# Three-operation weight decoding: a separate tile for signs and low bits, GpSimd as first reader, earlier release of raw tiles, and weights stored tile by tile

## The chip, the cores and the metric

The kernel runs on one core of one Trainium2 chip. The metric is the device time in microseconds (us) of one execution. TensorE (PE) does the matmuls, VectorE (DVE), ScalarE (ACT) and GpSimd (POOL) the elementwise work, and SyncE (SP) issues the DMA transfers.

## What is computed

Attention with a memory term, then two feed-forward blocks, on 2304 tokens of width 512:

```python
scores = softmax(causal(q @ k.T / 8))          # 4 batches, 8 heads, 576 tokens, 64 wide
attn = g * (phi(q) @ M_prev) / (phi(q) @ z_prev) + (1 - g) * (scores @ v)
x = attn.transpose(0, 2, 1, 3).reshape(2304, 512)
x = (((x @ w1) * (x @ w2)) @ w3) @ w_out       # d_ff = 1024
h = x @ w_in                                   # d_ff = 2048
out = (h - np.tanh(h)) @ wo2
```

All inputs but the weights are float32; the weights come as float64 (the scale factors promote them), as 64-bit words in memory. The kernel therefore decodes each float64 into float32 on the chip, and splits that into a rounded high part and a low rest, so that a product costs three fast matmuls (high by high, high by low, low by high).

## The kernel before

**Stages.** In the first some 260 us the attention runs: 80 units (16 head pairs by 5 query blocks), each scores on PE, row maximum on DVE, exponential on ACT, scaling on POOL (line 369), transposes and products on PE. Beside it, as background work, w3 and w_out are folded into one matrix (`fold_work`), which takes 24 decoded weight tiles. Then come six groups of 384 tokens (`for g in range(6)`): for each of eight column blocks f, PE forms `x @ w1` and `x @ w2` (tile ab), ACT copies (line 652), DVE multiplies (653), ACT rounds (656), DVE takes the rest (657), and PE multiplies by the folded matrix two blocks later (`x2_pe`, tile x). The memory term of the next group (`mem_group`, tile mw) runs beside them on all engines. From about 620 us the last block runs: 96 steps of `h2_pe` and `out_pe`.

**Decoding.** 72 tiles of 128 by 512 weights are decoded by `dec_ops`, a generator whose `yield`s cut it into steps. A raw tile holds the 64-bit words; `hw` is the upper half of each word, `lw` the lower, so both are read with 8 bytes from one element to the next. Before the change a tile takes: ACT scales `hw` into tile T (line 77) and writes rounded low bits, 16 bits each, into the raw tile (78); POOL clamps T (80) and writes the sign, again 16 bits each, into the raw tile (81); DVE shifts T by three and ORs it with the raw word (85). For a "whole" item this ends in the destination. For the others, POOL rounds to the high part (97) and DVE or POOL subtracts (100).

**Decoders.** A `Decoder` holds a list of items, steps up to `width` of them in turn, and calls `load` (SP issues the transfer, line 68) while items loaded and active are fewer than `ahead`. There are four: that of the fold (width 1, ahead 3), `wd` for w1 and w2 (16 items; width 2, ahead 3; the first four early, the rest in the first token group, where PE's block f asks for items 2f and 2f+1), `pre` for 24 whole items of the last block (width 2, ahead 2; 14 of them in the first two groups, ten later), and `fd` for its last eight (width 2, ahead 2, after 570 us). Raw tiles have three buffers, T two.

**Order.** The instructions are laid out by a list scheduler at build time, which takes the program's order as priority and gives tiles their buffers; on the chip each engine then works through its own fixed list in order, and SP's list of transfers is fixed too.

Of the kernel before, what the change touches and what calls it, by code (L numbers as in the profile page):

```python
# [11 lines left out]
F32 = mybir.dt.float32  # L12
F32R = mybir.dt.float32r
BF16 = mybir.dt.bfloat16
U32 = mybir.dt.uint32
U16 = mybir.dt.uint16
F16 = mybir.dt.float16
I64 = mybir.dt.int64
AF = mybir.ActivationFunctionType
ALU = mybir.AluOpType  # L20
# [1 line left out]
PSUM = bass.MemoryType.PSUM  # L22

REBIAS = 2.0 ** -112
TOP = float(np.uint32((255 << 20) - 1).view(np.float32))
LOW_SCALE, LOW_BIAS = 0.89 * 2.0 ** -29, 0.375


# [6 lines left out]
def block_kernel(ctx, tc, qk, qt, vt, mp, zp_d, beta, w1, w2, w3t, wo, wi, wo2, ident_d, mask_d, out):  # L35
    nc = tc.nc
    PE, DV, AC, PO, SP = nc.tensor, nc.vector, nc.scalar, nc.gpsimd, nc.sync
# [6 lines left out]
    zp = ctx.enter_context(tc.tile_pool(name="zp", bufs=1, side="right"))  # L44
    stg = {"raw": ctx.enter_context(tc.tile_pool(name="draw", bufs=3, side="right")),
           "T": ctx.enter_context(tc.tile_pool(name="dT", bufs=2, side="right"))}


    ident = cp.tile([128, 128], F32, name="ident")
    identb = cp.tile([128, 128], BF16, name="identb")  # L50
    maskb = cp.tile([128, 192], BF16, name="maskb")
    gates = cp.tile([128, 8], F32, name="gates")
    omg = cp.tile([128, 8], F32, name="omg")
    omgt = cp.tile([128, 4], F32, name="omgt")
# [7 lines left out]

    def dec_load(src):
        raw = stg["raw"].tile([128, 512], I64, tag="raw", name="raw")
        dst = raw[:]
        if len(src.shape) == 3:
            dst = dst.rearrange("p (k n) -> p k n", k=src.shape[1])
        SP.dma_start(out=dst, in_=src)
        return raw

    def dec_ops(raw, dst, lo_on, whole, hip):
        r16 = raw[:].bitcast(U16).rearrange("p (n t) -> p n t", t=4)
        rb = raw[:].bitcast(U32).rearrange("p (n t) -> p n t", t=2)
        lw, hw = rb[:, :, 0], rb[:, :, 1]
        t = stg["T"].tile([128, 512], U32, tag="T", name="T")
        tf = t[:].bitcast(F32)
        AC.activation(out=tf, in_=hw.bitcast(F32), func=AF.Copy, scale=REBIAS)  # L77
        AC.activation(out=r16[:, :, 0], in_=lw, func=AF.Copy, scale=LOW_SCALE, bias=LOW_BIAS)  # L78
        yield
        PO.tensor_scalar(out=tf, in0=tf, scalar1=TOP, scalar2=-TOP, op0=ALU.min, op1=ALU.max)  # L80
        PO.tensor_scalar(out=r16[:, :, 1].bitcast(F16), in0=hw.bitcast(F32), scalar1=2.0 ** -100, scalar2=2.0 ** -53,  # L81
                         op0=ALU.mult, op1=ALU.mult)
        yield
        o = dst() if whole else t[:]
        DV.scalar_tensor_tensor(out=o, in0=t, scalar=3, in1=lw,
                                op0=ALU.logical_shift_left, op1=ALU.bitwise_or)
        if whole:
            return
        yield
        hi, lo = dst()  # L90
        nhi[0] += 1
        if hip == 3:
            hip = nhi[0] % 2
        if hip == 2:
            DV.tensor_copy(out=hi, in_=tf)
        elif hip:
            PO.tensor_scalar(out=hi, in0=tf, scalar1=1.0, scalar2=1.0, op0=ALU.mult, op1=ALU.mult)
        else:
            AC.activation(out=hi, in_=tf, func=AF.Copy)
        lo_on.tensor_tensor(out=lo, in0=tf, in1=hi.bitcast(F32), op=ALU.subtract)  # L100

    class Decoder:


        def __init__(self, items, width, ahead, lo_on=DV, whole=False, hip=None):
            self.todo, self.loaded, self.active = deque(items), deque(), deque()
            self.width, self.ahead, self.done, self.total, self.lo_on = width, ahead, 0, len(self.todo), lo_on
            self.whole, self.hip = whole, HIP if hip is None else hip
            self.load()

        def load(self):
            while self.todo and len(self.loaded) + len(self.active) < self.ahead:
                src, dst = self.todo.popleft()
                self.loaded.append((dec_load(src), dst))

        def step(self):
            while self.loaded and len(self.active) < self.width:
                raw, dst = self.loaded.popleft()
                self.active.append(dec_ops(raw, dst, self.lo_on, self.whole, self.hip))
            if not self.active:  # L120
                return False
            gen = self.active.popleft()
            if next(gen, 1) is None:
                self.active.append(gen)
            else:
                self.done += 1
                self.load()
            return True

        def pump(self, n):  # L130
# [44 lines left out]
    for x in PA:  # L175
        apl[x] = att.enter_context(tc.tile_pool(name="ap" + x, bufs={"1": 1, "2": 2, "r": RB,
                                                                     "3": 1 if PU else PB, "4": 6}[x]))
    ap1, ap2, apr, ap3, ap4 = [apl[x] for x in "12r34"]
    V = [ap1.tile([128, 5, 2, 64], F32, name=f"v{i}") for i in range(2)]

    qk_t = {}
# [28 lines left out]
    def fold_o_item(j):  # L210
        def dst():
            FO[j] = slot(otags[j])
            return FO[j][:, 0], FO[j][:, 1]

        return wo[j * 128:j * 128 + 128], dst

    def fold_item(f, half):
        def dst():
            t = wslot(ap1, "zs")
            fv[f, half] = t  # L220
            return t[:, 0], t[:, 1]

        r = slice(512 * half, 512 * half + 512)
        return w3t[r, f * 128:f * 128 + 128].rearrange("(k p) c -> p k c", p=128), dst

    def fold_work(psum):
        seq = [("o", j) for j in range(4)]
# [39 lines left out]
    if True:  # L267
# [176 lines left out]
        def w_item(w, W, x, f):  # L444
            def dst():
                W[f] = slot(f"{x}{f}")
                return W[f][:, 0], W[f][:, 1]

            return w[:, f * 128:f * 128 + 128].rearrange("(k p) f -> p k f", p=128), dst

        wdec = [None]
        w_items = [w_item(w, W, x, f) for f in range(8) for w, W, x in ((w1, W1, "wa"), (w2, W2, "wb"))]
# [234 lines left out]
        pre_t = {}  # L687

        def fin_src(j):
            f = j // 2  # L690
            return (wo2[f * 128:f * 128 + 128] if j % 2
                    else wi[:, f * 128:f * 128 + 128].rearrange("(k p) f -> p k f", p=128))

        def fin_item(j):
            def dst():
                t = fslot(free.popleft())
                fin_tiles[j] = t[:, 0], t[:, 1]
                return fin_tiles[j]

            return fin_src(j), dst  # L700
# [50 lines left out]
        for g in range(6):  # L751
            for f in range(8):
                wd.until(2 * f + 2)
                o = ab_pe(xl, f)
                ab_chain(g, f, o)
                for y in [(g - 1, 7)] if f == 0 and g else [(g, 5), (g, 6)] if f == 7 else [(g, f - 2)] if f >= 2 else []:
                    x2_pe(*y)
                if f >= 1:
                    if g == 5:
                        if f == 1:  # L760
                            pre.until(2 * NF)
                            fd = Decoder([fin_item(j) for j in range(2 * NF, 32)], 2, 2, PO, False, HF)
                        left += [f"wa{f - 1}", f"wb{f - 1}"] + [f"wf{f - 3}"] * (f >= 3)
                        while plan and len(left) >= (2 if plan[0] == "P" else 1):
                            if plan.pop(0) == "P":
                                place(placed, [left.pop(0), left.pop(0)])
                                placed += 1
                            else:
                                give([left.pop(0)])
                    if g == 0:  # L770
                        wd.until(2 * f + 4)
                for _ in range(MS):
                    mem_step()
                if wd.done == 16:
                    if pre is None:
                        order = [*range(NZ), *range(NF, NF + NZ), *range(NZ, NF), *range(NF + NZ, 2 * NF)]
                        pre = Decoder([pre_item(j) for j in order], 2, 2, DV, True)
                    for _ in range(FS if g < 5 else FS5):
                        if pre.done < allowed:
                            pre.step()  # L780
                        elif fd and fd.done < given:
                            fd.step()
            if g + 1 < 6:
                mem_until(g + 1)
            xl = stage((g + 1) % 6)
        x2_pe(5, 7)
        pB.close()


        c2 = ctx.enter_context(tc.tile_pool(name="c2", bufs=2))  # L790
# [141 lines left out]

def layout(q, k, v, M_prev, z_prev, beta, moe_w1, moe_w2, moe_w3, moe_w_out, moe2_w_in, moe2_w_out):
    c = np.ascontiguousarray
    bits = lambda w: c(w).view(np.int64)
    ident = np.eye(128, dtype=np.float32)
    mask = np.zeros((128, 192), np.float32)
    mask[:, 0:128] = np.triu(np.full((128, 128), -1e30, np.float32), 1)
# [9 lines left out]
        "mp": c(M_prev).reshape(16, 128, 64),  # L948
        "zp": c(z_prev).reshape(4, 512),
        "beta": c(beta),  # L950
        "w1": bits(moe_w1),
        "w2": bits(moe_w2),
        "w3t": bits(moe_w3.T),
        "wo": bits(moe_w_out),
        "wi": bits(moe2_w_in),
        "wo2": bits(moe2_w_out),
        "ident": ident,
        "mask": mask,
    }
# [11 lines left out]
```

## Time and profile before

| | us |
|---|---|
| median of 3 runs | 1035.19 (1033.24 to 1036.75) |
| profiled execution, its own time | 1033.15 |
| its span in the trace | 1031.4 |

| engine | busy, share of the span |
|---|---|
| PE (matmul) | 976.2 us, 95% |
| DVE | 683.3 us, 66% |
| ACT | 673.5 us, 65% |
| POOL | 455.8 us, 44% |

The page gives the busy time of each engine; what it waited for, by whom, and when, comes from the views of waits, of order in time, and of stretches. PE's busy time is that of pipelined matmuls whose ends are modelled. The granted clock was between 0.97 and 1.00 of full speed in every stage below.

### The profile page before, as it was taken

The numbers are of one execution on the slowest core, as the hardware profiler recorded it, in microseconds if no ns is written. First come the engines' busy times: TensorE is split into PE (matmuls) and PEld (weight loads), VectorE is DVE, ScalarE is ACT, GpSimd is POOL, SyncE is SP. The second block draws the span as 40 slices with busy tenths as digits, with TensorE's granted clock in tenths as the row PEclk, the third lists the DMA queues.
The fourth block names the chain that finished last, engine by engine and source line by source line (L and its number), as shares of the span: only waits on it lengthen the run. The fifth ranks groups of instructions, "written<-read, shape, count | busy, mean of one in ns | idle before, by whom it ended". The sixth has DMA issues, their size and how long they took to land.

```text
span 1031.4 us, 15586 instructions
## 1 busy us (share of the span) xinstructions
PE 976.2 (95%) x5512; PEld 823.3 (80%) x5512; DVE 683.3 (66%) x1185; ACT 673.5 (65%) x1428; POOL 455.8 (44%) x500
## 2 busy tenths in 40 slices
PE   5899999988987988999999999999999999999998
PEld 2565566545776777999999999999999999989996
DVE  4755666876577666444221469878787888788875
ACT  6978977788445755337221568777786676777765
POOL 5866776776367666135100596222222222222221
PEclk9999999999999999999999999999999999999999
DMA  6444543441144443124000010000000000000000
GB/s 225 147 126 125 166 135 97 143 131 55 41 135 136 155 152 117 51 83 143 21 1 1 21 42 2 1 1 31 1 31 1 1 31 2 31 1 1 31 1 31
DMA packets 44238, 68.27 MB, mean 66 GB/s; under 512 B 4865, under 2 KB 30209, under 8 KB 44161
## 3 DMA queue, kind: packets, MB, share of 16 engines
q1 hardware_dynamic: 44160, 67.29, 20.4%
q8 instruction: 43, 0.70, 0.3%
q14 instruction: 35, 0.28, 0.1%
HBM read 62.56 MB, written 4.72 MB: 65 GB/s over the span
## 4 chain that ended last, share of the span: by engine, by line
PE 59%; DMA 4%; DVE 4%; ACT 2%; issue 1%; POOL 1%; DVEq 0%; SPq 0%; ACTq 0%; POOLq 0%
PE h L144 20%; PE o L144 19%; PE ab L144 12%; PE x L144 7%; DMA raw<-in_wi 2%; ACT raw L78 1%; DMA mw<-in_qt 1%; DVE mw L499 1%; DMA raw<-in_wo 1%; POOL raw L81 0%; DVE xs L529 0%; ACT abh L656 0%; DMA raw<-in_w 0%; DVE xl L633 0%; PE mo L512 0%
## 5 line engine op out<-in xcount | busy, mean ns | idle before, releaser
L858 POOL TENSOR_TENSOR gl<-s,gh 128x384 fp32r<-128x384 f32 x96 | 99.9, 1041 | 292.0 <-ACT gh L852 278.4
L78 ACT ACTIVATE raw<-raw 128x512 uint16<-128x512 uint32 x72 | 98.5, 1369 | 48.6 <-DMA raw<-in_wi 18.9
L81 POOL TENSOR_SCALAR raw<-raw 128x512 f16<-128x512 f32 x72 | 100.7, 1399 | 58.0 <-ACT raw L78 54.4
L144 PE MATMUL x<-abh,wf 128*128 128x384 f32 x384 | 108.8, 346 | 17.9 <-ACT abh L656 17.9
L144 PE MATMUL ab<-xh,wa 128*128 128x384 f32 x384 | 108.0, 340 | 3.4 <-DVE wa L100 1.4
L369 POOL TENSOR_SCALAR p<-p,st 128x128 f32<-128x128 f32 (+2 forms) x144 | 90.2, 639 | 42.4 <-DVE st L362 17.0
L144 PE MATMUL ab<-xh,wb 128*128 128x384 f32 x384 | 106.1, 336 | 0.0
L834 DVE SCALAR_TENSOR_TENSOR s<-s,u 128x384 f32<-128x384 f32 x96 | 84.7, 882 | 25.7 <-ACT s L824 24.6
L352 ACT ACTIVATE p<-sc,st 128x128 f32<-128x128 f32 (+2 forms) x144 | 78.5, 555 | 22.3 <-DVE st L343 19.5
L144 PE MATMUL sc<-r 64*64 64x288 f32 (+4 forms) x384 | 76.1, 486 | 16.1 <-ACT p L352 10.5
L830 ACT ACTIVATE u<-u,pc 128x384 f32<-128x384 f32 x96 | 59.5, 619 | 48.0 <-DVE s L834 48.0
L144 PEld LDWEIGHTS x<-abh,wf 128*128 128x128 f32 x384 | 71.3, 192 | 21.0 <-ACT abh L656 20.4
L653 DVE TENSOR_TENSOR a<-ab,a 128x384 f32<-128x384 f32 x48 | 26.6, 554 | 91.0 <-PE ab L144 76.4
L144 PEld LDWEIGHTS ab<-xh,wa 128*128 128x128 f32 x384 | 70.2, 188 | 7.3 <-DVE wa L100 1.7
L343 DVE TENSOR_REDUCE st<-sc 128x2 f32<-128x256 f32 (+4 forms) x80 | 63.4, 801 | 17.5 <-PE sc L144 17.3
L822 ACT ACTIVATE u<-h 128x384 f32<-128x384 f32 x96 | 46.9, 489 | 42.4 <-PE h L144 42.3
L840 DVE TENSOR_TENSOR t<-h,t 128x384 f32<-128x384 f32 x96 | 53.1, 553 | 26.3 <-ACT t L823 25.9
L144 PEld LDWEIGHTS ab<-xh,wb 128*128 128x128 f32 x384 | 70.0, 188 | 0.0
L839 DVE SCALAR_TENSOR_TENSOR s<-s,s 128x384 f32<-128x384 f32 x96 | 63.9, 666 | 8.3
L144 PE MATMUL x<-abl,wf 128*128 128x384 f32 x192 | 66.4, 346 | 0.3 <-DVE abl L657 0.3
L144 PE MATMUL ab<-xl,wa 128*128 128x384 f32 x192 | 65.0, 339 | 0.4 <-DVE xl L633 0.3
L80 POOL TENSOR_SCALAR T<-T 128x512 f32<-128x512 f32 x72 | 51.4, 714 | 30.5 <-ACT T L77 27.0
(214 smaller groups left out, 2614.7 us busy)
## 6 DMA issues: line engine op xcount, KB each, us to landing
raw<-in_wo SPq DMA_DIRECT2D x24, 512.0 KB, 3.5
r<-in_qk SPq DMA_DIRECT2D x15, 576.0 KB, 4.5
raw<-in_w3t SPq DMA_DIRECT2D x16, 512.0 KB, 3.6
raw<-in_w SPq DMA_DIRECT2D x16, 512.0 KB, 3.7
raw<-in_wi SPq DMA_DIRECT2D x16, 512.0 KB, 3.8
v<-in_vt SPq DMA_DIRECT2D x16, 320.0 KB, 3.4
mw<-in_qt SPq DMA_DIRECT2D x18, 256.0 KB, 2.7
out<-ob SPq DMA_DIRECT2D x18, 256.0 KB, 2.3
```

The source lines that it names most:

```text
L78: AC.activation(out=r16[:, :, 0], in_=lw, func=AF.Copy, scale=LOW_SCALE, bias=LOW_BIAS)
L80: PO.tensor_scalar(out=tf, in0=tf, scalar1=TOP, scalar2=-TOP, op0=ALU.min, op1=ALU.max)
L81: PO.tensor_scalar(out=r16[:, :, 1].bitcast(F16), in0=hw.bitcast(F32), scalar1=2.0 ** -100, scalar2=2.0 ** -53, op0=ALU.mult, op1=ALU.mult)
L144: return PE.matmul(o, lhsT, rhs, start=start, stop=stop).ins
L343: mark["V"][n] = DV.tensor_reduce(out=st[:, 0:2] if u < 4 else st[:, 0:1], in_=seen(n), axis=AX.X if u < 4 else AX.XY, op=ALU.max, negate= ...
L352: mark["A"][n] = AC.activation(out=p[:, x], in_=sc[:, x], func=AF.Exp, bias=st[:, x.start:x.start + 1], accum_out=st[:, 2 + x.start:3 + x. ...
L369: (DV if NV[u] == "V" else PO).tensor_scalar(out=pr, in0=pr, scalar1=sc, scalar2=1.0, op0=ALU.mult, op1=ALU.mult)
L830: AC.activation(out=u, in_=u, func=AF.Relu, bias=pc[:, 2:3])
L834: DV.scalar_tensor_tensor(out=s1, in0=s1, scalar=k2[0], in1=u, op0=ALU.add, op1=ALU.mult)
L839: DV.scalar_tensor_tensor(out=s1, in0=s2, scalar=k2[1], in1=s1, op0=ALU.add, op1=ALU.mult)
L840: DV.tensor_tensor(out=t, in0=o, in1=t, op=ALU.subtract)
L858: PO.tensor_tensor(out=l, in0=s1, in1=h[:].bitcast(F32), op=ALU.subtract)
```

## The change

The low bits and the sign no longer go into the raw tile. POOL first clamps `hw` straight from the raw tile into T. In the second step POOL multiplies `hw` by a tiny factor, so that only a signed zero remains, into a new tile E of whole 32-bit words; ACT scales T in place, and then writes the 16 low bits into the lower half of each word of E. After this step nothing reads the raw tile any more. DVE ORs T (shifted) with E. The decoder counts as `reading` only the items that have not got through the second step, and loads when that step is done. E has one buffer; the last decoder (`fd`) takes E out of T's two buffers, and its width goes from 2 to 1. To make room, two small constant tiles move to a pool that is closed after the attention. On the host the weights are stored tile by tile, so that every partition's 4 KB of a tile is contiguous; before, w1, w2, w3 and w_in came in four pieces of 1 KB.

```diff
-TOP = float(np.uint32((255 << 20) - 1).view(np.float32))
+TOP = float(np.uint32((1151 << 20) - 1).view(np.float32))
+    dE = ExitStack()
+    stg["E"] = dE.enter_context(tc.tile_pool(name="dE", bufs=1, side="right"))
...
     def dec_load(src):
         raw = stg["raw"].tile([128, 512], I64, tag="raw", name="raw")
-        dst = raw[:]
-        if len(src.shape) == 3:
-            dst = dst.rearrange("p (k n) -> p k n", k=src.shape[1])
-        SP.dma_start(out=dst, in_=src)
+        SP.dma_start(out=raw, in_=src)
...
-        AC.activation(out=tf, in_=hw.bitcast(F32), func=AF.Copy, scale=REBIAS)
-        AC.activation(out=r16[:, :, 0], in_=lw, func=AF.Copy, scale=LOW_SCALE, bias=LOW_BIAS)
+        PO.tensor_scalar(out=tf, in0=hw, scalar1=TOP, scalar2=-TOP, op0=ALU.min, op1=ALU.max)
         yield
-        PO.tensor_scalar(out=tf, in0=tf, scalar1=TOP, scalar2=-TOP, op0=ALU.min, op1=ALU.max)
-        PO.tensor_scalar(out=r16[:, :, 1].bitcast(F16), in0=hw.bitcast(F32), scalar1=2.0 ** -100, scalar2=2.0 ** -53,
+        e = stg[x].tile([128, 512], U32, tag=x, name="E")
+        PO.tensor_scalar(out=e[:].bitcast(F32), in0=hw, scalar1=2.0 ** -100, scalar2=2.0 ** -53,
                          op0=ALU.mult, op1=ALU.mult)
-        yield
+        AC.activation(out=tf, in_=tf, func=AF.Copy, scale=REBIAS)
+        e16 = e[:].bitcast(U16).rearrange("p (n t) -> p n t", t=2)[:, :, 0]
+        AC.activation(out=e16, in_=lw, func=AF.Copy, scale=LOW_SCALE, bias=LOW_BIAS)
+        yield 1
         o = dst() if whole else t[:]
-        DV.scalar_tensor_tensor(out=o, in0=t, scalar=3, in1=lw,
+        DV.scalar_tensor_tensor(out=o, in0=t, scalar=3, in1=e,
                                 op0=ALU.logical_shift_left, op1=ALU.bitwise_or)
...
         def load(self):
-            while self.todo and len(self.loaded) + len(self.active) < self.ahead:
+            while self.todo and len(self.loaded) + self.reading < self.ahead:
...
             while self.loaded and len(self.active) < self.width:
                 raw, dst = self.loaded.popleft()
+                self.reading += 1
...
-            if next(gen, 1) is None:
+            r = next(gen, 2)
+            if r == 1:
+                self.reading -= 1
+                self.load()
+            if r == 2:
+                self.done += 1
+            else:
                 self.active.append(gen)
-            else:
-                self.done += 1
-                self.load()
...
+    identb = ap1.tile([128, 128], BF16, name="identb")
+    maskb = ap1.tile([128, 192], BF16, name="maskb")
...
-                            fd = Decoder([fin_item(j) for j in range(2 * NF, 32)], 2, 2, PO, False, HF)
+                            fd = Decoder([fin_item(j) for j in range(2 * NF, 32)], 1, 2, PO, False, HF, "T")
...
         pB.close()
+        dE.close()
...
+    def cols(w):
+        return rows(w.reshape(4, 128, -1, 128).transpose(2, 1, 0, 3).reshape(-1, 512))
...
-        "w1": bits(moe_w1),
+        "w1": cols(moe_w1),
```

## Rows read from the trace of the kernel before

**Rows 1.** Stretches, us: length; busy of PE, PEld, DVE, ACT, POOL; clock; DMA

```profile
0.00:52.00 52.00, 37.89 (x227) 20.58 (x228) 29.91 (x66) 40.41 (x99) 34.02 (x53) 0.97 0.57 186
52.00:210.00 158.00, 150.26 (x976) 92.43 (x974) 102.52 (x220) 127.26 (x311) 112.58 (x149) 1.00 0.41 129
210.00:285.00 75.00, 69.54 (x482) 44.23 (x482) 49.86 (x117) 51.34 (x134) 44.01 (x58) 0.98 0.26 78
285.00:345.00 60.00, 46.30 (x266) 40.98 (x265) 44.30 (x67) 32.55 (x52) 40.64 (x40) 0.97 0.44 139
345.00:420.00 75.00, 66.39 (x378) 60.53 (x378) 50.36 (x84) 43.97 (x72) 45.09 (x40) 0.98 0.43 135
420.00:1032.00 612.00, 605.85 (x3196) 564.54 (x3192) 406.33 (x635) 377.99 (x764) 179.45 (x164) 1.00 0.07 23
```

**Rows 2.** Waits of PE, 285 to 420 us: total us, times, longest us

```profile
PE x L144 <- ACT abh L656: 17.9, 8, 4.8
PE ab L144 <- DVE wa L100: 1.4, 1, 1.4
```

**Rows 3.** Waits of ACT for raw tiles, 285 to 420 us

```profile
ACT raw L78 <- DMA raw<-in_w: 10.7, 4, 4.8
ACT raw L78 <- DMA raw<-in_wi: 10.4, 8, 2.1
ACT raw L78 <- DMA raw<-in_wo: 6.4, 5, 2.0
```

**Rows 4.** Order in time, PE: start, length, what; in brackets idle before, releaser

```profile
312.16 1.65 PE L144 MATMUL x<-abh,wf 128*128 128x384 f32 x4 [4.76 <-ACT abh L656]
...
331.88 0.96 PE L144 MATMUL x<-abh,wf 128*128 128x384 f32 x4 [1.61 <-ACT abh L656]
...
397.38 1.65 PE L144 MATMUL x<-abh,wf 128*128 128x384 f32 x4 [3.39 <-ACT abh L656]
```

**Rows 5.** Order in time, ACT

```profile
328.49 1.37 ACT L78 ACTIVATE raw<-raw 128x512 uint16<-128x512 uint32 x1 [2.13 <-DMA raw<-in_wi]
...
395.66 1.35 ACT L78 ACTIVATE raw<-raw 128x512 uint16<-128x512 uint32 x1 [1.81 <-DMA raw<-in_wi]
```

**Rows 6.** Chain that ended last, 300 to 314 us: start, length, what

```profile
305.25 1.07 DVE T L85
...
306.38 3.96 DMA raw<-in_w
...
310.44 1.35 ACT raw L78
311.79 0.33 ACT abh L656
```

**Rows 7.** Instructions of lines 77 to 85 and 497: ns shortest/median/longest; first, last start

```profile
L77 ACT ACTIVATE T<-raw x72: 648/677/738, 10.2 to 621.9; 128x512 f32<-128x512 f32 x72
L78 ACT ACTIVATE raw<-raw x72: 1323/1368/1443, 10.8 to 603.1; 128x512 uint16<-128x512 uint32 x72
L80 POOL TENSOR_SCALAR T<-T x72: 614/617/1123, 10.9 to 624.4; 128x512 f32<-128x512 f32 x72
L81 POOL TENSOR_SCALAR raw<-raw x72: 1326/1356/1879, 12.2 to 605.3; 128x512 f16<-128x512 f32 x72
L85 DVE SCALAR_TENSOR_TENSOR T<-T,raw x48: 677/693/1792, 13.6 to 627.3; 128x512 uint32<-128x512 uint32 x48
...
L497 ACT ACTIVATE mw<-mw x18: 612/632/687, 187.2 to 436.4; 128x512 f32<-128x512 f32 x18
```

**Rows 8.** DMA issues of the page: count, KB each, median us to landing

```profile
raw<-in_wo SPq DMA_DIRECT2D x24, 512.0 KB, 3.5
...
raw<-in_wi SPq DMA_DIRECT2D x16, 512.0 KB, 3.8
```

**Rows 9.** Waits of ACT for raw tiles, 52 to 210 us

```profile
ACT raw L78 <- DMA raw<-in_w: 1.2, 1, 1.2
```

**Rows 10.** Instructions of line 81, 285 to 420 us

```profile
L81 POOL TENSOR_SCALAR raw<-raw x24: 1327/1359/1864, 289.9 to 401.5; 128x512 f16<-128x512 f32 x24
```

**Rows 11.** Matmuls of tile h by tiles z

```profile
L144 PE MATMUL h<-xh,z x144: 333/335/346, 669.4 to 1013.8; 128*128 128x384 f32 x144
```

More of the change, by code (lines that the diff above doesn't have):

```diff
@@ L16 @@
 U16 = mybir.dt.uint16
-F16 = mybir.dt.float16
 I64 = mybir.dt.int64
@@ L46, in block_kernel @@
            "T": ctx.enter_context(tc.tile_pool(name="dT", bufs=2, side="right"))}
+    dE = ExitStack()
+    stg["E"] = dE.enter_context(tc.tile_pool(name="dE", bufs=1, side="right"))
     ident = cp.tile([128, 128], F32, name="ident")
-    identb = cp.tile([128, 128], BF16, name="identb")
-    maskb = cp.tile([128, 192], BF16, name="maskb")
     gates = cp.tile([128, 8], F32, name="gates")
@@ L64, in dec_load, with dec_ops @@
         raw = stg["raw"].tile([128, 512], I64, tag="raw", name="raw")
-        dst = raw[:]
-        if len(src.shape) == 3:
-            dst = dst.rearrange("p (k n) -> p k n", k=src.shape[1])
-        SP.dma_start(out=dst, in_=src)
-        return raw
-    def dec_ops(raw, dst, lo_on, whole, hip):
-        r16 = raw[:].bitcast(U16).rearrange("p (n t) -> p n t", t=4)
+        SP.dma_start(out=raw, in_=src)
+        return raw
+    def dec_ops(raw, dst, lo_on, whole, hip, x):
         rb = raw[:].bitcast(U32).rearrange("p (n t) -> p n t", t=2)
-        lw, hw = rb[:, :, 0], rb[:, :, 1]
+        lw, hw = rb[:, :, 0], rb[:, :, 1].bitcast(F32)
         t = stg["T"].tile([128, 512], U32, tag="T", name="T")
         tf = t[:].bitcast(F32)
-        AC.activation(out=tf, in_=hw.bitcast(F32), func=AF.Copy, scale=REBIAS)
-        AC.activation(out=r16[:, :, 0], in_=lw, func=AF.Copy, scale=LOW_SCALE, bias=LOW_BIAS)
+        PO.tensor_scalar(out=tf, in0=hw, scalar1=TOP, scalar2=-TOP, op0=ALU.min, op1=ALU.max)
         yield
-        PO.tensor_scalar(out=tf, in0=tf, scalar1=TOP, scalar2=-TOP, op0=ALU.min, op1=ALU.max)
-        PO.tensor_scalar(out=r16[:, :, 1].bitcast(F16), in0=hw.bitcast(F32), scalar1=2.0 ** -100, scalar2=2.0 ** -53,
+        e = stg[x].tile([128, 512], U32, tag=x, name="E")
+        PO.tensor_scalar(out=e[:].bitcast(F32), in0=hw, scalar1=2.0 ** -100, scalar2=2.0 ** -53,
                          op0=ALU.mult, op1=ALU.mult)
-        yield
+        AC.activation(out=tf, in_=tf, func=AF.Copy, scale=REBIAS)
+        e16 = e[:].bitcast(U16).rearrange("p (n t) -> p n t", t=2)[:, :, 0]
+        AC.activation(out=e16, in_=lw, func=AF.Copy, scale=LOW_SCALE, bias=LOW_BIAS)
+        yield 1
         o = dst() if whole else t[:]
-        DV.scalar_tensor_tensor(out=o, in0=t, scalar=3, in1=lw,
+        DV.scalar_tensor_tensor(out=o, in0=t, scalar=3, in1=e,
                                 op0=ALU.logical_shift_left, op1=ALU.bitwise_or)
@@ L102, in block_kernel, with __init__ @@
     class Decoder:
-        def __init__(self, items, width, ahead, lo_on=DV, whole=False, hip=None):
+        def __init__(self, items, width, ahead, lo_on=DV, whole=False, hip=None, x="E"):
             self.todo, self.loaded, self.active = deque(items), deque(), deque()
             self.width, self.ahead, self.done, self.total, self.lo_on = width, ahead, 0, len(self.todo), lo_on
-            self.whole, self.hip = whole, HIP if hip is None else hip
+            self.whole, self.hip, self.reading = whole, HIP if hip is None else hip, 0
+            self.x = x
             self.load()
         def load(self):
-            while self.todo and len(self.loaded) + len(self.active) < self.ahead:
+            while self.todo and len(self.loaded) + self.reading < self.ahead:
                 src, dst = self.todo.popleft()
@@ L118, in step @@
                 raw, dst = self.loaded.popleft()
-                self.active.append(dec_ops(raw, dst, self.lo_on, self.whole, self.hip))
+                self.reading += 1
+                self.active.append(dec_ops(raw, dst, self.lo_on, self.whole, self.hip, self.x))
             if not self.active:
@@ L213, in dst @@
             return FO[j][:, 0], FO[j][:, 1]
-        return wo[j * 128:j * 128 + 128], dst
+        return wo[j], dst
     def fold_item(f, half):
@@ L221, in dst @@
             return t[:, 0], t[:, 1]
-        r = slice(512 * half, 512 * half + 512)
-        return w3t[r, f * 128:f * 128 + 128].rearrange("(k p) c -> p k c", p=128), dst
+        return w3t[8 * half + f], dst
     def fold_work(psum):
@@ L447, in dst @@
                 return W[f][:, 0], W[f][:, 1]
-            return w[:, f * 128:f * 128 + 128].rearrange("(k p) f -> p k f", p=128), dst
+            return w[f], dst
         wdec = [None]
@@ L689, in fin_src @@
         def fin_src(j):
-            f = j // 2
-            return (wo2[f * 128:f * 128 + 128] if j % 2
-                    else wi[:, f * 128:f * 128 + 128].rearrange("(k p) f -> p k f", p=128))
+            return (wo2 if j % 2 else wi)[j // 2]
         def fin_item(j):
@@ L934, in layout, with rows @@
     c = np.ascontiguousarray
-    bits = lambda w: c(w).view(np.int64)
+    def rows(w):
+        return c(w).view(np.int64).reshape(-1, 128, 512)
+    def cols(w):
+        return rows(w.reshape(4, 128, -1, 128).transpose(2, 1, 0, 3).reshape(-1, 512))
     ident = np.eye(128, dtype=np.float32)
@@ L950, in layout @@
         "beta": c(beta),
-        "w1": bits(moe_w1),
[L952 to L956, printed above, removed]
+        "w1": cols(moe_w1),
+        "w2": cols(moe_w2),
+        "w3t": np.concatenate([cols(moe_w3.T[:512]), cols(moe_w3.T[512:])]),
+        "wo": rows(moe_w_out),
+        "wi": cols(moe2_w_in),
+        "wo2": rows(moe2_w_out),
         "ident": ident,
```

## Prediction, made blind

> **What bounds the kernel now.** I read the busy times of the page first, then PE by stretches, then PE's waits in the stretch that loses most, then who held the engine that PE waited for. PE is busy for 976.2 of 1031.4 us. The stretches [rows 1] show where the other 55 us lie, as length less PE's busy time: 14.1 to 52 us, 7.7 from there to 210, 5.5 to 285, 13.7 from 285 to 345, 8.6 to 420, and 6.2 in all of the last 612 (0.6 of which is past the end). So a change in decoding can only earn what PE loses in the first 420 us, some 49 us; after that PE has nothing to gain.
>
> From 285 to 420 us PE loses 22.3 us, and 17.9 of them are eight waits of tile x for ACT's rounding of abh [rows 2]. ACT is busy there for little over half of the time [rows 1], so it isn't short of time; it stands. In the same stretch it stands 27.5 us, in 17 waits, for raw tiles to land [rows 3]. ACT works in order, so the copy and the rounding that PE needs stand behind such a wait. Three of PE's eight waits can be followed to one: 4.76, 1.61 and 3.39 us, 9.8 in all [rows 4]. At 312.16 us the chain tells the whole story [rows 6]: DVE's OR gives the raw buffer back at 306.3, the transfer starts at 306.4 and takes 3.96 us, ACT's low-bits copy takes 1.35, then comes abh, then PE. The other two have the same wait of ACT shortly before them, 2.13 and 1.81 us [rows 5]. One more wait of PE, 1.4 us, is for a decoded tile wa itself [rows 2]. The remaining 8.1 us of the x waits (17.9 less 9.8) I put down to DVE's queue, through which abh's input goes.
>
> **The change, part by part.** *The operations.* Before, a tile costs ACT 0.68 + 1.37 us, POOL 0.62 + 1.36, DVE 0.69 [rows 7]. After, POOL's clamp reads words 8 bytes apart and writes them packed. The trace has no such POOL operation. Its ends are 0.62 (line 80, packed both ways) and 1.36 (line 81, the same read but a 16-bit write 8 bytes apart). I take 0.62, because ACT, which also takes twice as long for its 16-bit write (1.37), reads the same words 8 bytes apart in line 77 for 0.68 against 0.63 packed (line 497): the read costs next to nothing, the narrow write doubles [rows 7]. The sign operation becomes the same kind, again 0.62, ends as before. ACT's scaling goes from 0.68 to some 0.63. Its low-bits copy still writes 16 bits, now 4 bytes apart: 1.37 if the width counts, 0.68 if the spacing did; I take 1.37. DVE's OR reads E packed: 0.69 as before, no row says otherwise. So a tile loses 0.74 us on POOL (1.97 to 1.23), ends from -0.74 to +0.74, and nothing much elsewhere; 72 tiles, 53 us less of POOL.
>
> [...]
>
> *The raw tile.* It was held until DVE's OR, and the next load was called when the item was done. Now it is free after ACT's low-bits copy of step two, and the items in their third and fourth steps don't count against `ahead`. With `wd` (ahead 3) all three buffers can be landed or under way while two items are in their late steps; with `pre` (ahead 2) two can. At 4.85 us between tiles (23 gaps in 111.6 us [rows 10]) one whole tile of lead covers a landing of 3.5 to 3.8 us [rows 8]. Hence the 9.8 us of PE's waits for ACT behind a landing should mostly go: ends 0 and 9.8, I take 8, and 1 of the 1.4 for wa. SP's list is in order, so each raw load that goes earlier also stands ahead of a load of mw or mc that it used to follow; an issue is under 0.4 us, and I cost it at nothing under that lead.
>
> *Who waits first.* POOL's clamp now carries the wait for the landing, and ACT's scaling waits for POOL. Behind the clamp on POOL are line 369's scaling in the attention, lines 500 and 508 of the memory term, and the high parts of other tiles. In the attention this is cheap: from 52 to 210 us ACT stood only 1.2 us for a raw tile [rows 9].
>
> *DVE's queue.* The OR ranges from 0.68 to 1.79 us for one form [rows 7]; it is longest where POOL works at the same time. With POOL's part of a tile down from 1.97 to 1.23, I take 2.5 of the 8.1 us; ends 0 and 8.1. [...]
>
> *The first 285 us.* PE loses 27.3 us there. 33 of 72 tiles fall into it (72 less the 24 of [rows 10] and 15 later), so POOL is relieved by 24 us of 191 [rows 1]. PE's waits there are mostly for the attention's own chain, so I take 4, ends -5 (POOL's new place ahead of line 369) and +10.
>
> *The layout.* Rows of 4 KB land in 3.5 us, pieces of 1 KB in 3.8 [rows 8]: 0.3 us for 48 tiles, hidden once the lead is there. *The last decoder* goes one tile at a time: 0.62 + 0.62 + 0.63 + 1.37 + 0.69 + 0.62 + some 1.4 for the subtraction on POOL is 6 us, eight tiles 48 us. Now the last OR starts at 627.3 [rows 7] and the first such tile is used at 669.4 [rows 11]; the 42 us between hide it, and PE is full there anyway.
>
> The sum: 8 + 1 + 2.5 + 4 = 15.5 us off the profiled 1033.15 is 1017.7. That execution is 2.0 us under the median of 1035.19; the runs spread by more, so I write 1018, between 1017.7 and 1019.7.
>
> **The rivals.** *The full gain.* All three sums at their better ends, 9.8 + 1.4 + 8.1 + 10 = 29.3: 1004. For it speaks that one cause feeds all; against it that the memory term's chain, next in line, was not touched. *A wait that only moves.* ACT now waits for POOL, which waits for the raw tile or for the single buffer of E; half of the landing waits stay, and the attention gains nothing: 5 + 1 = 6, so 1029. *No earlier loads.* Where SP's list holds raw loads behind those of mw that wait for their own tiles, the lead isn't there, and the change doesn't do what it says: 1034. *Slower, by the one tile E.* In `wd` and `pre` two items are in flight, but E is held from POOL's sign to DVE's OR: 0.62 + 1.37 + 0.69 = 2.7 us bare, and the second item's sign waits for the first one's OR. Against 4.85 us per tile now [rows 10] this is harmless until the two handovers add more than 2.2 us a tile. At 6 us per tile the ten tiles of `wd` among the 24 (14 are `pre`'s and have time) come 1.15 us later each, 12 us in all, and PE waits for wa: 1047. For it speaks that an engine's list had waits of several us at each handover [rows 3], against it that the old hold of T was longer than E's is.
>
> **How the numbers follow.** Forecast 48%, its own range 1010 to 1026; full gain 10%; moved wait 17%; no earlier loads 12%; slower by E 13%. The likeliest is 1018. The range 1004 to 1037 leaves out the slower rival and the edge of the full gain. 0.3% (3 us) is about what a measurement of this kernel can tell from no change: faster 48 + 10 + 17 = 75%, same 12%, slower 13%.
>
> **What would show it.** Right: POOL's first two operations at about 0.62 us each; ACT's waits for landings gone from 285 to 420 us and PE's waits for abh there down from 17.9 to under 10; POOL some 50 us less busy; the last 600 us unchanged. Wrong: POOL's operations near 1.36; ACT's waits for POOL as long as those for landings were; POOL's sign waiting for DVE's OR, and PE for wa, in the first token group; longer waits of line 369 in the attention.

## The result and the profile after

| | before | after |
|---|---|---|
| median of 4 runs, us | 1034.58 (1033.24 to 1036.75) | 1004.70 (1004.53 to 1005.39) |
| profiled execution, us (span) | 1033.15 (1031.4) | 1005.39 (1003.6) |

The ratio is 0.9711, with a 95% interval of 0.9692 to 0.9729: 2.9% faster, some 30 us. The forecast was 1018, with 1004 to 1037 as its range, so the sign was right and the size was little more than half of what came.

The stretches of the changed kernel, with the columns of [rows 1]:

```profile
0.00:52.00 52.00, 42.21 (x257) 24.09 (x259) 31.36 (x71) 38.88 (x107) 34.71 (x59) 1.00 0.59 198
52.00:210.00 158.00, 152.84 (x987) 92.07 (x981) 104.61 (x228) 116.89 (x316) 98.36 (x148) 1.00 0.40 130
210.00:285.00 75.00, 71.80 (x497) 50.45 (x498) 51.69 (x116) 50.01 (x130) 44.89 (x59) 1.00 0.29 95
285.00:345.00 60.00, 54.58 (x299) 46.14 (x298) 40.75 (x76) 28.77 (x56) 37.10 (x42) 0.97 0.47 148
345.00:420.00 75.00, 74.76 (x451) 70.47 (x450) 44.72 (x88) 33.93 (x70) 31.37 (x34) 1.00 0.37 118
420.00:1032.00 612.00, 578.87 (x3032) 539.25 (x3029) 388.41 (x608) 365.44 (x753) 161.82 (x161) 1.00 0.06 21
```

PE's idle time (length less busy) was 14.1, 7.7, 5.5, 13.7 and 8.6 us in the first five stretches and is 9.8, 5.2, 3.2, 5.4 and 0.2 us. Over the whole span it falls from 55.2 (1031.4 less 976.2) to 28.5 us (1003.6 less 975.1). The span falls by 27.8, so nearly all of the gain is idle time of PE: 9 us of it in the first 285 us and 17 from 285 to 420. The stretches are cut at the same times in both; work has moved forward across them.

The waits of PE from 285 to 420 us, against [rows 2]:

```profile
PE x L146 <- ACT abh L659: 3.4, 2, 2.6
PE x L146 <- DVE abl L660: 1.2, 1, 1.2
PE ab L146 <- ACT xh L635: 0.6, 1, 0.6
```

The wait for abh went from 17.9 us in eight to 3.4 in two, and that for wa is gone. In this stretch ACT no longer waits for any landing of a raw tile (27.5 us in [rows 3]).

The decoding instructions of the changed kernel, with the columns of [rows 7]:

```profile
L72 POOL TENSOR_SCALAR T<-raw x72: 635/652/1047, 10.1 to 598.9; 128x512 f32<-128x512 f32 x72
...
L75 POOL TENSOR_SCALAR E<-raw x72: 639/662/1177, 10.8 to 603.4; 128x512 f32<-128x512 f32 x72
...
L77 ACT ACTIVATE T<-T x72: 604/625/669, 11.2 to 599.6; 128x512 f32<-128x512 f32 x72
...
L79 ACT ACTIVATE E<-raw x72: 767/785/837, 11.7 to 604.9; 128x512 uint16<-128x512 uint32 x72
...
L82 DVE SCALAR_TENSOR_TENSOR T<-T,E x48: 637/693/1743, 12.5 to 606.5; 128x512 uint32<-128x512 uint32 x48
```

The sign operation fell from 1.36 to 0.66 us, near the 0.62 that was taken. The low-bits copy fell from 1.37 to 0.79 us, where 1.37 was taken. What is called the chain of a tile below is the bare sum of the operations that follow each other from the raw words to the OR, without the waits between them. It is now clamp, sign, low bits, OR: 0.65 + 0.66 + 0.79 + 0.69 = 2.79 us. (The sign doesn't need the clamp, but stands behind it on POOL for 71 of the 72 tiles.) Before, it was low bits, sign, OR, 1.37 + 1.36 + 0.69 = 3.42 us, and 4.10 where the scaling (0.68) went ahead of the low bits on ACT [rows 7], as it did for 21 of the 72 tiles. These two counts take the first instruction of each line as the first tile's, the second as the second's, and so on.

### The profile page after: what moved, and what is told of

The parts are those of the page before. It is cut to its first block, busy times and chain, and to the rows that moved or that the text cites. A ratio compares the mean times of both kernels' runs of the same rounds, so it can differ in the third digit from the quotient of the medians.

```text
span 1003.6 us, 15463 instructions
## 1 busy us (share of the span) xinstructions
PE 975.1 (97%) x5512; PEld 822.5 (82%) x5512; DVE 661.5 (66%) x1185; ACT 633.9 (63%) x1428; POOL 408.2 (41%) x500
## 4 chain that ended last, share of the span: by engine, by line
PE 85%; ACT 5%; DVE 4%; DMA 2%; POOL 2%; issue 1%; SPq 0%; DVEq 0%; ACTq 0%; POOLq 0%
PE o L146 24%; PE h L146 20%; PE ab L146 17%; PE x L146 9%; PE sc L146 5%; PE fo L146 5%; PE t L404 3%; ACT p L355 2%; PE mo L146 2%; DMA mw<-in_qt 1%; DVE st L346 1%; DMA r<-in_qk 1%; ACT g L383 1%; ACT E L79 1%; POOL E L75 1%
## 5 line engine op out<-in xcount | busy, mean ns | idle before, releaser
L146 PE MATMUL x<-abh,wf 128*128 128x384 f32 x384 | 106.3, 341 | 3.4 <-ACT abh L659 3.4
L75 POOL TENSOR_SCALAR E<-raw 128x512 f32<-128x512 f32 x72 | 55.0, 764 | 43.4 <-DVE z2p L82 8.6
L655 ACT ACTIVATE a<-ab 128x384 f32<-128x384 f32 x48 | 23.5, 489 | 75.4 <-PE ab L146 75.4
L72 POOL TENSOR_SCALAR T<-raw 128x512 f32<-128x512 f32 x72 | 51.4, 714 | 41.0 <-DVE zs L97 8.7
```

The source lines that it names most:

```text
L72: PO.tensor_scalar(out=tf, in0=hw, scalar1=TOP, scalar2=-TOP, op0=ALU.min, op1=ALU.max)
L75: PO.tensor_scalar(out=e[:].bitcast(F32), in0=hw, scalar1=2.0 ** -100, scalar2=2.0 ** -53, op0=ALU.mult, op1=ALU.mult)
L146: return PE.matmul(o, lhsT, rhs, start=start, stop=stop).ins
```

## The experiments

Three theories were set against each other. *Lead*, the blind one: raw tiles are asked for earlier, so nobody stands for a landing. *Work*: the operations are shorter. *Order*: POOL, not ACT, stands in front of the landing. All runs below have at least four executions, and each ratio is to runs of the kernel before on the same chip.

**The load rule put back.**

```diff
-            while self.todo and len(self.loaded) + self.reading < self.ahead:
+            while self.todo and len(self.loaded) + len(self.active) < self.ahead:
...
                 self.reading -= 1
-                self.load()
             if r == 2:
                 self.done += 1
+                self.load()
```

> The changed kernel with the old rule for loading: an item's successor is loaded when the item is done, and all active items count against the limit. Operations, tiles and layout stay. Lead theory (the gain is that raw tiles are asked for one tile earlier): the waits for landings come back, on GpSimd now, and some 17 of the 30 us are lost, about 1020 us. Work theory (the gain is the shorter operations): 1005 to 1009 us. Order theory (the gain is that GpSimd, not ScalarE, stands in front of the landing): 1005 to 1010 us, with the landing waits in GpSimd's rows and none in ScalarE's.

Measured: 1004.77 us, ratio 0.9692 (0.9661 to 0.9724): nothing is lost. PE's wait for abh from 285 to 420 us is the same 3.4 us. The earlier call of the load earns nothing by itself. But the edit moved no load, so the run doesn't test the lead theory. What SP's loads of raw tiles waited for most shows it, first in the kernel before, then in the changed kernel, then in this one:

```profile
SPq L68 <- DVE T L85: 237.0, 34, 98.0
```

```profile
SPq L64 <- ACT E L79: 272.8, 49, 94.7
```

```profile
SPq L64 <- ACT E L79: 272.3, 49, 94.7
```

In the changed kernel 68 of the 69 loads after the first three go out within 0.2 us of the end of the low-bits copy that read the tile three loads earlier, and one goes out 45.4 us after it, at 271.8 us; in this one SP's waits for that copy are the same to 0.5 us. Before, a load waited in this way for DVE's OR. So here the three raw buffers set when a load starts, not the rule. The raw tile's earlier release, which comes with E, is in this run as it is in the changed kernel. What tests the lead is further down: the kernel with both operations twice, and the one with two raw tiles.

As the next three kernels ran on the same chip, this 1004.77 is also what they are compared with.

**The time put back, on ACT, on POOL, and on both.** The second copy of each operation writes what the first one wrote.

```diff
+        AC.activation(out=e16, in_=lw, func=AF.Copy, scale=LOW_SCALE, bias=LOW_BIAS)    # on ACT
+        PO.tensor_scalar(out=e[:].bitcast(F32), in0=hw, scalar1=2.0 ** -100, scalar2=2.0 ** -53,
+                         op0=ALU.mult, op1=ALU.mult)                                    # on POOL
```

> The changed kernel with ScalarE's low-bits copy done twice, so that a tile costs ScalarE 0.63 + 2 x 0.79 = 2.20 us, against 2.05 before the change and 1.41 after it. Work theory: a good part of the gain goes, 1014 us or more. Lead and order theories: 1005 to 1009 us, since ScalarE is busy for 63% only.

> The changed kernel with GpSimd's sign operation done twice, so that a tile costs GpSimd 1.97 us before the high part, as before the change. Work theory: 1012 us or more, with longer waits of the attention for line 372 and more long operations on VectorE. Lead and order theories: 1005 to 1009 us.

> The changed kernel with both the low-bits copy and the sign operation done twice: GpSimd's and ScalarE's work per tile is that of before, order, lead and layout are the new ones. Work theory: most of the gain is gone, 1025 us or more. Lead and order theories together: 1005 to 1013 us.

| kernel | chain of a tile, us | measured, us | ratio to before |
|---|---|---|---|
| load rule put back | 2.79 | 1004.77 | 0.9692 (0.9661 to 0.9724) |
| sign twice | 3.45 | 1014.98 | 0.9789 (0.9759 to 0.9820) |
| low bits twice | 3.58 | 1022.68 | 0.9861 (0.9826 to 0.9896) |
| both twice | 4.24 | 1032.51 | 0.9962 (0.9944 to 0.9979) |

The chain is 2.79 us plus the second copies: 0.66 us (sign) and 0.79 us (low bits). With both, 1.45 us more per tile costs 27.7 us, and the time is within 0.4% of the kernel before, although order, load rule, layout and tile E are the new ones. (ACT's work is then 0.15 us a tile above that of before, so a little too much is put back.) The two alone cost 10.2 and 17.9 us, which add up to 28.1. So neither the order nor the raw tile's early release keeps the gain when the time is back. That is one half of the work theory; the other half, whether the short operations bring the gain without the new order, is the next run's.

Where the time goes can be read from the stretches. With both twice they are, up to 420 us and with the columns of [rows 1]:

```profile
0.00:52.00 52.00, 38.59 (x221) 20.65 (x222) 27.73 (x66) 38.43 (x102) 33.55 (x59) 0.97 0.53 177
52.00:210.00 158.00, 150.00 (x958) 92.04 (x957) 102.33 (x212) 124.05 (x320) 105.52 (x160) 1.00 0.38 123
210.00:285.00 75.00, 68.58 (x487) 42.49 (x486) 51.25 (x122) 54.91 (x148) 48.43 (x68) 1.00 0.30 96
285.00:345.00 60.00, 49.46 (x259) 42.98 (x258) 36.41 (x62) 29.31 (x52) 40.66 (x47) 0.91 0.41 124
345.00:420.00 75.00, 71.62 (x417) 64.94 (x415) 45.46 (x86) 44.20 (x85) 39.52 (x47) 1.00 0.36 119
```

| PE's idle time (length less busy), us | to 285 us | 285 to 420 us |
|---|---|---|
| before | 27.3 | 22.3 |
| changed | 18.2 | 5.7 |
| sign twice | 20.0 | 11.7 |
| low bits twice | 25.6 | 11.2 |
| both twice | 27.8 | 13.9 |

With both twice the gain of the first 285 us is gone, but from 285 to 420 us half of it stays, and PE's wait for abh there is 5.6 us, not 17.9. Of the 25.6 us by which the span is longer than the changed kernel's (1029.2 against 1003.6), 6.3 are longer busy time of PE (981.4 against 975.1). So the total comes back, but not all of it in the waits that were there before.

The run also tells what the missing landing waits were worth. With both twice, the only wait for a landing on ACT or POOL in the whole trace is

```profile
POOL T L72 <- DMA raw<-in_wo: 2.8, 1, 2.8
```

against 51.4 us on ACT before,

```profile
ACT raw L78 <- DMA raw<-in_wi: 18.9, 12, 2.5
ACT raw L78 <- DMA raw<-in_wo: 15.8, 11, 2.9
ACT raw L78 <- DMA raw<-in_w: 11.9, 5, 4.8
ACT T L77 <- DMA raw<-in_wi: 3.1, 1, 3.1
ACT T L77 <- DMA raw<-in_wo: 1.7, 1, 1.7
```

and the kernel is still about as slow as before.

**The short operations alone, in the old order.** The kernel before with tile E; ACT scales first, the old load rule, the old layout.

```diff
+        AC.activation(out=tf, in_=hw, func=AF.Copy, scale=REBIAS)
         yield
+        PO.tensor_scalar(out=tf, in0=tf, scalar1=TOP, scalar2=-TOP, op0=ALU.min, op1=ALU.max)
         e = stg[x].tile([128, 512], U32, tag=x, name="E")
         PO.tensor_scalar(out=e[:].bitcast(F32), in0=hw, scalar1=2.0 ** -100, scalar2=2.0 ** -53,
                          op0=ALU.mult, op1=ALU.mult)
-        AC.activation(out=tf, in_=tf, func=AF.Copy, scale=REBIAS)
```

> The kernel before with the short operations alone: tile E takes GpSimd's signed zeros and ScalarE's low bits, and the last decoder goes one tile at a time with E out of T's buffers. ScalarE is still the first reader (it scales the raw words into T), the rule for loading and the layout of the weights are the old ones. Work theory: nearly the whole gain, 1005 to 1012 us (the old layout alone cost some 3 us). Order theory (GpSimd in front of the landing is needed too): 1018 us or more, and ScalarE's waits for landings stay at 20 us or more from 285 to 420 us.

Measured: 1009.07 us, ratio 0.9727 (0.9700 to 0.9753). Nearly the whole gain is there (0.9711 for the changed kernel). ACT is the first reader again, and yet it waits for landings from 285 to 420 us only this long:

```profile
ACT T L75 <- DMA raw<-in_wo: 0.8, 1, 0.8
...
ACT T L75 <- DMA raw<-in_wi: 0.5, 1, 0.5
```

So POOL as first reader isn't needed either, and the order theory falls with its own number (20 us of waits or more). Two limits: the low-bits copy is the raw tile's last reader here too, so its earlier release came along with the short operations. And the chain sums don't order this kernel: POOL takes the sign ahead of the clamp for 32 of the 72 tiles, and the sum is then 0.67 + 0.79 + 0.69 = 2.15 us; where the clamp goes first it is 0.67 + 0.62 + 0.67 + 0.79 + 0.69 = 3.44. The time is that of the changed kernel in the old layout (1008.35 us, below), whose chain is 2.79.

**Time on ACT beside the chain.**

```diff
         AC.activation(out=e16, in_=lw, func=AF.Copy, scale=LOW_SCALE, bias=LOW_BIAS)
+        for _ in range(4):
+            AC.activation(out=omg, in_=omg, func=AF.Copy)
```

> The changed kernel with four small in-place copies of a 128x8 tile on ScalarE behind each tile's low-bits copy, some 0.8 us per tile. Nothing waits for their results. If ScalarE's occupied time is what counts, the loss is that of the second low-bits copy: 1018 to 1024 us. If the length of the decode chain counts (the second low-bits copy stood between raw tile and OR, these don't): 1005 to 1010 us.

Measured: 1008.38 us, ratio 0.9726 (0.9697 to 0.9754), 2 us by the ratios or 4 by the medians above the changed kernel. ACT is busy for 672.7 us, 38.8 more than in the changed kernel; the second low-bits copy made it 681.1 and cost 18 us. Here busy time of ACT whose results nothing used counted little, and a link in the chain counted. A limit of this run: the scheduler placed the small copies where it saw room, as these stretches show against those of the changed kernel (ACT is the fourth number after the length: 67.15 against 50.01, then 33.62 against 33.93).

```profile
210.00:285.00 75.00, 69.77 (x484) 47.84 (x483) 51.18 (x115) 67.15 (x258) 42.57 (x57) 1.00 0.28 89
...
345.00:420.00 75.00, 74.51 (x449) 69.87 (x447) 44.97 (x90) 33.62 (x69) 32.77 (x35) 1.00 0.41 124
```

**The signs as whole words in the raw tile, without E.** With the old load rule.

```diff
-        PO.tensor_scalar(out=e[:].bitcast(F32), in0=hw, scalar1=2.0 ** -100, scalar2=2.0 ** -53,
+        PO.tensor_scalar(out=hw, in0=hw, scalar1=2.0 ** -100, scalar2=2.0 ** -53,
...
-        e16 = e[:].bitcast(U16).rearrange("p (n t) -> p n t", t=2)[:, :, 0]
+        e16 = raw[:].bitcast(U16).rearrange("p (n t) -> p n t", t=4)[:, :, 2]
...
-        DV.scalar_tensor_tensor(out=o, in0=t, scalar=3, in1=e,
+        DV.scalar_tensor_tensor(out=o, in0=t, scalar=3, in1=rb[:, :, 1],
```

> The changed kernel without tile E: GpSimd writes the signed zero as a whole 32-bit word back into the upper half of the raw word, ScalarE writes the low bits into that word's lower half, VectorE reads it there. The raw tile is held until VectorE's OR, as before the change, and the old rule for loading is used; GpSimd is still the first reader. Prices: a whole word 8 bytes apart shows whether width or spacing doubled the sign operation (0.66 us if width, 1.36 if spacing), and the low-bits copy goes back to 1.37 us if spacing did it. Lead theory: 1020 us or more. Order theory: 1005 to 1012 us. Work theory: between, some 1015 us.

Measured: 1030.32 us, ratio 0.9948 (0.9929 to 0.9967). Its two rows give the price of a write:

```profile
L74 POOL TENSOR_SCALAR raw<-raw x72: 638/664/1180, 12.7 to 617.3; 128x512 f32<-128x512 f32 x72
L78 ACT ACTIVATE raw<-raw x72: 1324/1366/1442, 15.1 to 621.2; 128x512 uint16<-128x512 uint32 x72
```

A whole word written 8 bytes apart costs POOL 0.66 us, no more than a packed one; 16 bits 8 bytes apart cost ACT 1.37 us, and 4 bytes apart 0.79. The chain is 0.65 + 0.66 + 1.37 + 0.69 = 3.37 us, so by the table above some 1015 to 1020 us were due. It is 10 us or more slower than that, and 9.3 us of its time above the changed kernel is longer busy time of PE (984.4 against 975.1 us), which the chain doesn't explain. Against the kernel before it gains only 5.7 us by the medians. What it has beside the longer copy is the raw tile held until the OR.

**The raw tile held until the OR, with short operations.**

```diff
         DV.scalar_tensor_tensor(out=o, in0=t, scalar=3, in1=e,
                                 op0=ALU.logical_shift_left, op1=ALU.bitwise_or)
+        DV.tensor_copy(out=omg[:, 0:1], in_=rb[:, 0:1, 1].bitcast(F32))
```

> The changed kernel in which the raw tile is held until after VectorE's OR, as before the change: behind each OR, VectorE copies one column of the raw tile into a spare column (some 0.1 us), and the old rule for loading is used. E, the short operations, the order and the layout stay. Chain theory (what counts is how long a tile takes from raw words to OR; raw to OR is as short as in the changed kernel): 1005 to 1009 us. Release theory (the 1030 us of the kernel with signs in place come from the raw tile's long hold, not from its 1.37 us copy): 1016 us or more.

Measured: 1011.90 us, ratio 0.9767 (0.9734 to 0.9800), between the two expectations. The run doesn't decide, because the scheduler put the copy, which needs only the raw tile, ahead of the OR. So it stood on DVE for the landings instead:

```profile
DVE omg L84 <- DMA raw<-in_wo: 14.2, 11, 2.8
...
DVE omg L84 <- DMA raw<-in_wi: 9.9, 9, 2.1
...
DVE omg L84 <- DMA raw<-in_w: 5.2, 7, 1.2
```

What it does show is that 29.3 us of standing for landings on DVE, put in on purpose, together with the old load rule and 72 copies of 0.15 us, costs 7 us. What a hold of every raw tile until the OR is worth stays open; the next run takes one of the three raw tiles away instead.

**Two tiles E, two raw tiles.**

```diff
-    stg = {"raw": ctx.enter_context(tc.tile_pool(name="draw", bufs=3, side="right")),
+    stg = {"raw": ctx.enter_context(tc.tile_pool(name="draw", bufs=2, side="right")),
...
-    stg["E"] = dE.enter_context(tc.tile_pool(name="dE", bufs=1, side="right"))
+    stg["E"] = dE.enter_context(tc.tile_pool(name="dE", bufs=2, side="right"))
```

> The changed kernel with two buffers of E instead of one and, to make room, two of the raw tile instead of three. Lead theory: one raw tile fewer brings waits for landings back, 1008 us or more. Rival of the single E (GpSimd's sign waits for the other tile's OR): those waits go and PE's last waits in the first token groups with them, 1000 us or less. If neither matters: within 3 us of the changed kernel, 1002 to 1008 us.

Measured: 1007.78 us, ratio 0.9720 (0.9694 to 0.9745), 0 to 3 us more than the changed kernel. POOL now stands for landings, over the whole run:

```profile
POOL T L72 <- DMA raw<-in_wo: 16.7, 10, 4.5
...
POOL E L75 <- DMA raw<-in_w: 7.1, 6, 2.4
POOL E L75 <- DMA raw<-in_w3t: 7.0, 6, 2.3
POOL T L72 <- DMA raw<-in_wi: 6.9, 6, 2.2
...
POOL E L75 <- DMA raw<-in_wo: 3.4, 2, 1.8
```

That is 41.1 us in 30 waits, and the kernel is no more than 3 us slower. So the lead that the third raw tile gives is worth little here, unless the second E earned back what it cost: what a second E beside three raw tiles is worth wasn't tried.

**The layout alone, and the layout undone.** The first is the kernel before with the six weight arrays stored tile by tile, the second the changed kernel with the old arrays and loads.

```diff
-        "w1": bits(moe_w1),
+        "w1": cols(moe_w1),
```

> The kernel before with the new layout of the weights alone. If pieces of 4 KB rather than 1 KB matter only by the 0.2 to 0.3 us of each landing: within 3 us of before, 1032 to 1035 us. If the 18400 packets fewer relieve the queue that the loads of the memory term share: 1025 us or less.

> The changed kernel with the old layout of the weights, in four pieces of 1 KB per partition. Lead theory: the lead covers 0.3 us more of a landing, so 1004 to 1007 us. If the layout carries part of the gain: 1010 us or more.

Measured: 1033.92 us, ratio 0.9988 (0.9971 to 1.0004), no difference that can be told; and 1008.35 us, ratio 0.9742 (0.9718 to 0.9766), some 3 us slower than the changed kernel, at the edge of what can be told.

**One tile of lead in the kernel before.**

```diff
-                        pre = Decoder([pre_item(j) for j in order], 2, 2, DV, True)
+                        pre = Decoder([pre_item(j) for j in order], 2, 3, DV, True)
```

> The kernel before with one number changed: the decoder of whole items may have three items loaded and active rather than two, so it loads one tile earlier; nothing else. Lead theory: the 14.5 us that ScalarE stood for landings from 345 to 420 us go for the most part, and 5 to 9 us are gained there: 1026 to 1030 us. Work and order theories: 1032 to 1036 us.

Measured: 1035.91 us, ratio 1.0007 (0.9987 to 1.0027): nothing. ACT's waits for landings from 285 to 420 us are nearly those of [rows 3], and PE's wait for abh is 17.3 us:

```profile
ACT raw L78 <- DMA raw<-in_wi: 10.7, 8, 2.0
...
ACT raw L78 <- DMA raw<-in_w: 8.3, 3, 4.8
ACT raw L78 <- DMA raw<-in_wo: 6.5, 6, 2.1
```

So this knob gave no lead at all, and the run says nothing on what a lead would be worth; the three raw buffers were held as before.

## Why the prediction was right in sign and short in size

**What bounds the kernel.** Right: PE's idle time before 420 us was all there was to gain. It fell by 25.8 us there (49.6 to 23.8), and by 0.8 us after.

**The operations.** Right for POOL: 0.62 was taken twice, and 0.65 and 0.66 came. The low-bits copy is the term that was mis-sized. Its two ends were 1.37 and 0.68, and the choice of 1.37 rested on the width of the write. Neither end came: 0.79 us at 4 bytes against 1.37 at 8, so the spacing counts for this 16-bit write of ACT. (The tile written is another one too, E instead of the raw tile; for POOL's whole words that made no difference, 0.66 us in either.) So a tile lost 0.58 us on ACT that the sum had at nothing, 42 us over 72 tiles. By the run with the low bits twice, 0.79 us more on this link is worth 17.9 us, so 0.58 are worth some 13 (an estimate by proportion). POOL's 0.66 us less per tile, which the run with the sign twice puts back exactly, are worth 10.2 us, where the sum had 6.5 (2.5 for DVE's queue and 4 for the first 285 us). Together that is 23 of the 30 us; the layout may hold another 3. These shares are read from the changed kernel's side; from the other side, the kernel without E has POOL's short operation and gains 5.7 us. That the read costs next to nothing held as far as it was tried: reads 8 bytes apart with packed writes take POOL 0.65 us, against 0.62 packed [rows 7]. No run here has reads further apart.

**The lead.** This step failed, in its reason. Of the 15.5 us, 8 were put on raw tiles that come earlier. The landing waits of ACT did go, and PE's waits for abh with them. But with the operations' time put back the landing waits stay away while the time returns, and with two raw tiles 41.1 us of such waits return at 0 to 3 us. The step was wrong in its means too: the new load rule moved no load. Loads start earlier in a tile's life because the low-bits copy, not the OR, gives the raw buffer back. The chain of [rows 6] was read rightly as an order of events, and wrongly as a price: had the transfer landed sooner, the tile would still have needed its 3.4 to 4.1 us of operations on ACT, POOL and DVE. Why ACT stood at all has a likely reason in the lists: its low-bits copy needed no other tile than the raw one and so was placed right at the landing, while the new first operation needs a buffer of T. That is argued, not shown.

**Who waits first, and DVE's queue.** The clamp's waits for landings are 1.4 us from 285 to 420 us, as cheap as was taken. The OR's median is 0.69 us before and after; DVE's busy time fell from 683.3 to 661.5 us. ORs of over 0.9 us are 22 of 72 before and 16 of 72 after. All of them overlap an operation of POOL in time, while the 25 before and the 29 after that overlap none take 0.69 us at most. What the drop from 22 to 16 is worth no run separates, and the 2.5 us taken for DVE's queue remain the author's estimate; with both operations twice DVE's busy time is still down, at 667.4 us, and the gain is gone.

**The first 285 us.** 4 us were taken, with an end at 10; PE's idle time fell by 9.1 (27.3 to 18.2). By the table of idle times, the sign done twice costs some 2 us there and the low bits done twice some 7. So the sum was right that POOL's relief earns little in the attention; what it lacked is the shorter low-bits copy, which it had at its old price.

**The layout and the last decoder.** The layout was costed at nothing, and it is within 3 us. The last decoder's OR now starts at 606.5 us at the latest, and PE's last 584 us (1003.6 less 420) have 4.7 us of idle time, so it stayed hidden.

**The rivals.** The full gain (1004) is what came in time, though not for its reasons; it had been given 10%, and the measured time is 0.7 us inside the lower end of the stated range, so that it lies there owes something to luck. The single E does make POOL wait, 33.9 us in 15 waits over the run, but it didn't decide: two E with two raw tiles bought nothing. The rival of no earlier loads was right about the rule and wrong about the time. That the waits only move was seen in part: with two raw tiles they moved to POOL, at no price.

What stays open: how much of the gain needs the raw tile's earlier release, which every fast kernel here has, and which is not enough by itself (both twice has it); whether it is the length of the chain from raw words to OR that PE feels or the place of these links in the engines' lists, since every edit of a chain also moves the list; and the 10 us by which the kernel without E is slower than its chain says.

## What to carry to other kernels

A wait for a transfer on the chain that ended last isn't yet what the transfer costs: put the operations' time back, or put a wait in on purpose, before the gain is credited to one of them. And before a knob is taken as tested, look in the trace whether it moved what it should move: here two edits of the load rule left the loads where the buffers had them. In a decode that several engines share, count the microseconds that one tile needs from engine to engine; here each of them, added to the changed kernel, cost some 19 us over 72 tiles (27.7 us for 1.45), while 38.8 us of ACT's busy time beside the chain cost 2 to 4. The sum of a chain is a hint and no more: two kernels here don't follow it. When a 16-bit strided write appears in such a chain, look for a form that writes whole words, or 16 bits at a smaller spacing: here POOL's went from 1.36 to 0.66 us by the first, and ACT's from 1.37 to 0.79 by the second.

## What the runs showed of the hardware

Writes of 128 by 512 elements, read 8 bytes apart: ACT takes 0.68 us for packed words [rows 7], 0.79 for 16 bits 4 bytes apart (the changed kernel), 1.37 for 16 bits 8 bytes apart ([rows 7], and the kernel without E). POOL takes 0.65 and 0.66 for packed words (the changed kernel), 0.66 for words 8 bytes apart (the kernel without E), and 1.36 for 16 bits 8 bytes apart [rows 7]. That POOL's whole words cost the same at either spacing, while ACT's narrow write costs 0.58 us more at the wider one, was not expected.
